# Packing two heads into 4-byte words for the transposes of q, with decay rates through the array, spare matmuls at the start and half-width last stores

## The chip, the cores and the metric

The kernel runs on one core of one Trainium2 chip. The metric is the device time of one execution in microseconds (us). A profile gives, for one execution, a span that is about 1.9 us shorter than that time. In the text PE is the matmul engine (TensorE), PEld its weight load, DVE is VectorE, ACT is ScalarE, POOL is GpSimd and SP is the engine that issues the loads and stores. "The array" is PE's array.

## The reference

An attention without a softmax over scores, followed by a gated recurrence. Sizes: 8 batches, 8 heads, 576 rows, 64 columns a head; 512 model columns and 512 inner columns. The layout changes are cut.

```python
q_s = exp(q - max) / sum over the 64 columns        # per row and head
k_s = exp(k - max) / sum over the 576 rows          # per column and head
kv  = einsum('bhsd,bhse->bhde', k_s, v)             # 64 x 64 per head
x   = einsum('bhsd,bhde->bhse', q_s, kv)            # then (batch, row, 512)
val, gate = split(x @ w_in)                         # 512 -> 512 + 512
h = exp(A_log) * h + val[:, t]                      # scan over the rows, per batch
out = (silu(gate) * ys) @ w_out
```

## The kernel before

All work is written down as one list of operations, `ORDER`. Each engine takes its own operations from it in that order, so a wait of one operation holds all later ones of that engine. A token such as `norm/P.2.0` is the operation `norm` on POOL for batch 2, part 0. Buffers are rings: a tile's memory is free when the tile so many places back has been read.

The rows of all batches are one sequence of 4608, cut into nine chunks of 512. Chunk 0 needs x of batch 0, chunk 1 needs x of batches 0 and 1, chunk 2 of batches 1 and 2. For each batch the steps are: load q, k, v; exponent of q and k on ACT (`expq`, `expk`); sums of q on DVE (`qsum`); normalization (`norm`); transposes on PE (`transp`) and their copy out of PSUM (`tevac`); k times v (`kv`), normalized on DVE (`kvn`); x products (`xa` twice, `xr` for the last rows) with copies into `xT`. For each chunk: projections (`val`, `gate`), `scan` on DVE, `tanh` on ACT, two products, output matmuls and stores.

```python
RINGS = {"qf": 2, "kf": 2, "vf": 2, "eq": 2, ..., "tp": 1, "ax": 1, "pp": 3, "po": 2, ...}

def lalog(self, e):      # 512 reads of 4 bytes
    nc.sync.dma_start(out=alog, in_=moe_A_log.rearrange("(m p) -> p m", p=128))

def expq(self, e, b, q2):
    nc.scalar.activation(buf("eq", b)[:, q2].rearrange("p c h d -> p h c d"),
        buf("qf", b)[:, 2*q2:2*q2+2].rearrange("p h (c d) -> p h c d", c=C), AF.Exp)

def transp(self, e, b, g):
    tp = buf("tp", (b, g))
    src = buf("eq", b).rearrange("p q c h d -> p (q c) (h d)")
    for j in range(6):
        nc.tensor.transpose(tp[:, j, :], src[:, 6*g + j, :], ident)      # bf16, 128 x 128

def xa(self, e, b, q2):                     # "ax": one accumulation buffer of two banks
    xp, kvc, eqT = buf("ax", (b, q2)), buf("kvc", b), buf("eqT", b)
    for h2 in range(2):
        for hp2 in range(2):
            r = slice(hp2*64, hp2*64 + 64)
            nc.tensor.matmul(xp[h2*64:h2*64+64, hp2, 0:C*PA]...,
                             lhsT=kvc[r, h2, q2, :], rhs=eqT[r, q2, :, h2, 0:PA], ...)

def scan(self, e, i, m):
    nc.vector.tensor_tensor_scan(buf("y", (i, m)), a, buf("pp", ("v", i, m)), init, ...)

for op in ORDER.split():                    # engines take their work in this order
    ...
# ... (the rest is cut)
```

## Time and profile before

| | before |
|---|---|
| time, median of 3 runs | 149.74 us (149.5 to 150.08) |
| span of the profile | 147.8 us |
| first projection | 22.63 us |
| first projection of chunk 2; PE is full from here | 53.85 us |
| end of the last matmul | 144.07 us |

The profile's page gives busy time and slices; the prediction below shows the lines that carry it. Each line says: source line, engine, operation, what it writes and reads, size, count, then busy us, mean ns of one, and idle time of the engine just before.

```profile
L265 PE MATMUL tp<-ident,eq 128*128 128x128 bf16 x144 | 13.8, 238 | 14.9 <-POOL eq L257 11.0
...
L229 ACT ACTIVATE eq<-qf 128x1152 bf16<-128x1152 f32 x16 | 18.2, 1163 | 7.1 <-DMA qf<-in_q_dram 7.1
```

The mean of a transpose, 238 ns, is not what one costs: six of them follow each other in 0.34 us, 56 ns each. An exponent of q (1152 elements per partition) takes ACT 1163 ns. The starts of the first sixteen projection matmuls (512 columns) are 427 ns apart from 23.0 to 27.3 us, and 216 ns apart from 27.6 us on.

### The profile page before, as it was taken

The numbers are of one execution on the slowest core, as the hardware profiler recorded it, in microseconds if no ns is written. First come the engines' busy times: TensorE is split into PE (matmuls) and PEld (weight loads), VectorE is DVE, ScalarE is ACT, GpSimd is POOL, SyncE is SP. The second block draws the span as 40 slices with busy tenths as digits, with TensorE's granted clock in tenths as the row PEclk, the third lists the DMA queues.
The fourth block names the chain that finished last, engine by engine and source line by source line (L and its number), as shares of the span: only waits on it lengthen the run. The fifth ranks groups of instructions, "written<-read, shape, count | busy, mean of one in ns | idle before, by whom it ended". The sixth has DMA issues, their size and how long they took to land.

```text
span 147.8 us, 3234 instructions
## 1 busy us (share of the span) xinstructions
PE 122.9 (83%) x1312; PEld 62.7 (42%) x1312; DVE 118.5 (80%) x141; ACT 101.5 (69%) x142; POOL 92.9 (63%) x77
## 2 busy tenths in 40 slices
PE   0022498949696999999999999999999999999990
PEld 0011353423352445445446776644534444444430
DVE  0498773899896798999989998897998999998510
ACT  3619756799696789799898978898555224444641
POOL 2050760979999999999998997893430660153300
PEclk9999999999999999999999999999999999999998
DMA  4999999999999999999999996000703042305296
GB/s 131 409 394 390 325 398 390 388 391 389 390 392 392 391 391 391 399 397 395 405 399 408 398 395 258 4 0 0 282 6 142 0 176 108 146 0 205 81 343 227
DMA packets 19887, 41.11 MB, mean 278 GB/s; under 512 B 1440, under 2 KB 1440, under 8 KB 19872
## 3 DMA queue, kind: packets, MB, share of 16 engines
q1 hardware_dynamic: 19872, 40.90, 74.0%
q8 instruction: 10, 0.16, 0.4%
q14 instruction: 5, 0.04, 0.1%
HBM read 31.46 MB, written 9.44 MB: 277 GB/s over the span
## 4 chain that ended last, share of the span: by engine, by line
PE 59%; DMA 16%; DVE 8%; POOL 7%; ACT 5%; issue 2%; SPq 1%; ACTq 0%
PE pp L356 32%; PE po L390 18%; DMA qf<-in_q_dram 16%; PE tp L265 3%; POOL eq L257 3%; ACT eq L229 3%; DVE y L370 2%; PE ax L317 2%; DVE z L382 2%; DVE qs L249 2%; PE ax L278 2%; POOL vb L186 2%; POOL z L382 1%; DVE u L378 1%; PE pp L390 1%
## 5 line engine op out<-in xcount | busy, mean ns | idle before, releaser
L356 PE MATMUL pp<-xT,win 128*128 128x512 bf16 (+1 forms) x320 | 70.8, 367 | 1.6 <-ACT xT L184 0.7
L382 POOL TENSOR_TENSOR z<-u,y 128x512 bf16<-128x512 f32 x28 | 35.8, 1298 | 25.8 <-DVE u L378 16.1
L356 PEld LDWEIGHTS <-win 128*128 128x128 bf16 x320 | 30.5, 99 | 33.3 <-issue 5.9
L370 DVE TENSOR_TENSOR_SCAN y<-decay,y,pp 128x512 f32<-128x512 f32 x32 | 40.4, 1271 | 2.6 <-PE pp L356 2.5
L390 PE MATMUL po<-wout,z 128*128 128x512 bf16 x136 | 34.0, 379 | 1.1 <-POOL z L382 0.9
L257 POOL TENSOR_TENSOR eq<-eq,qs 128x1152 bf16<-128x1152 bf16 x14 | 29.9, 2150 | 7.1 <-DVE qs L252 5.9
L375 ACT ACTIVATE th<-pp 128x512 f32<-128x512 f32 x36 | 21.4, 600 | 17.3 <-PE pp L356 16.0
L378 DVE SCALAR_TENSOR_TENSOR u<-th,pp 128x512 f32<-128x512 f32 x36 | 24.1, 677 | 4.5 <-ACT th L375 3.7
L265 PE MATMUL tp<-ident,eq 128*128 128x128 bf16 x144 | 13.8, 238 | 14.9 <-POOL eq L257 11.0
L249 DVE TENSOR_REDUCE qs<-eq 128x36 f32<-128x2304 bf16 (+1 forms) x10 | 20.5, 2054 | 6.2 <-ACT eq L229 6.2
L229 ACT ACTIVATE eq<-qf 128x1152 bf16<-128x1152 f32 x16 | 18.2, 1163 | 7.1 <-DMA qf<-in_q_dram 7.1
L186 POOL CAST vb<-vf 128x1152 bf16<-128x1152 f32 (+1 forms) x14 | 15.9, 1162 | 9.9 <-DMA vf<-in_v_dram 9.9
L184 ACT ACTIVATE ob<-po 128x512 f32<-128x512 f32 x27 | 16.0, 600 | 7.8 <-PE po L390 7.8
L390 PEld LDWEIGHTS <-z 128*128 128x128 bf16 x144 | 13.5, 98 | 16.3 <-POOL z L382 1.8
L265 PEld LDWEIGHTS <-eq 128*128 128x128 bf16 x144 | 10.4, 106 | 19.6 <-POOL eq L257 11.7
L235 ACT ACTIVATE ek<-kf 128x2304 bf16<-128x2304 f32 (+1 forms) x10 | 17.3, 1734 | 0.0
L184 ACT ACTIVATE xT<-ax 128x1008 bf16<-128x1008 f32 (+1 forms) x12 | 11.8, 982 | 3.1 <-PE ax L300 2.1
L184 ACT ACTIVATE eqT<-tp 128x768 bf16<-128x768 bf16 x14 | 11.4, 814 | 1.0 <-PE tp L265 1.0
L278 PE MATMUL ax<-vb,ek 64*64 64x65 bf16 x576 | 7.3, 199 | 2.0 <-POOL vb L186 1.8
L278 PEld LDWEIGHTS <-ek 64*64 64x64 bf16 x576 | 6.2, 112 | 4.3 <-issue 2.4
L370 DVE TENSOR_TENSOR_SCAN y<-acol,pp 128x512 f32<-128x512 f32 x4 | 4.8, 1214 | 3.2 <-ACT decay L184 2.4
L382 DVE TENSOR_TENSOR z<-u,y 128x512 bf16<-128x512 f32 x8 | 7.0, 885 | 0.1
(37 smaller groups left out, 67.8 us busy)
## 6 DMA issues: line engine op xcount, KB each, us to landing
out_dram<-ob SPq DMA_DIRECT2D x16, 512.0 KB, 3.2
qf<-in_q_dram SPq DMA_DIRECT2D x7, 1152.0 KB, 13.3
kf<-in_k_dram SPq DMA_DIRECT2D x7, 1152.0 KB, 12.6
vf<-in_v_dram SPq DMA_DIRECT2D x7, 1152.0 KB, 12.5
y<-in_moe_w_in_dram SPq DMA_DIRECT2D x8, 256.0 KB, 11.2
qf<-in_q_dram SPq DMA_DIRECT2D x2, 576.0 KB, 4.3
kf<-in_k_dram SPq DMA_DIRECT2D x2, 576.0 KB, 8.0
vf<-in_v_dram SPq DMA_DIRECT2D x2, 576.0 KB, 10.3
```

The costliest lines, as they stand in the source:

```text
L184: nc.scalar.activation(out, in_, AF.Copy)
L186: eng[e].tensor_copy(out, in_)
L229: nc.scalar.activation(buf("eq", b)[:, q2].rearrange("p c h d -> p h c d"), buf("qf", b)[:, 2 * q2:2 * q2 + 2].rearrange("p h (c d) -> p h ...
L249: nc.vector.tensor_reduce(s[:, 0, n].rearrange("p (a o) -> p a o", o=1), buf("eq", b)[:, h].rearrange("p q c h d -> p (q c h) d"), axis=AX ...
L257: eng[e].tensor_tensor(x, x, r.rearrange("p (a o) -> p a o", o=1) .broadcast_to([128, 2 * C, D]), ALU.mult)
L265: nc.tensor.transpose(tp[:, j, :], src[:, 6 * g + j, :], ident)
L356: nc.tensor.matmul(dst[:, a:z], lhsT=win[:, kt, col:col + 128], rhs=xT[:, kt, s0:s0 + z - a], start=(kt == 0), stop=(kt == 3))
L370: nc.vector.tensor_tensor_scan(buf("y", (i, m)), a, buf("pp", ("v", i, m)), init, op0=ALU.mult, op1=ALU.add)
L375: nc.scalar.activation(buf("th", (i, m)), buf("pp", ("g", i, m)), AF.Tanh, scale=0.5)
L378: nc.vector.scalar_tensor_tensor(buf("u", (i, m)), buf("th", (i, m)), 1.0, buf("pp", ("g", i, m)), op0=ALU.add, op1=ALU.mult)
L382: eng[e].tensor_tensor(buf("z", i)[:, m], buf("u", (i, m)), buf("y", (i, m)), ALU.mult)
L390: nc.tensor.matmul(self._po(i, r), lhsT=buf("z", i)[:, m, r * 128:(r + 1) * 128], rhs=wout[:, m], start=(m == 0), stop=(m == NM - 1))
```

## The change

The intent has five parts.

1. Two heads are interleaved, so that two bf16 values are one 4-byte word. One transpose then moves two heads: 72 transposes of 4 bytes instead of 144 of 2 bytes. ACT's exponent of q writes with a step of 4 bytes, and the x products read with that step.
2. The decay rates are loaded as four rows of 512 bytes (`lalog`) and turned by a small transpose (`talog`).
3. The factor 0.5 moves from the conversion of w_out to the output copies.
4. 37 spare matmuls on zeros (`warm`) are to keep the array busy until the first chunk.
5. The order is new: gates of chunk 0 first, all of w_in loaded ahead of batch 1's k and v. One of the last output groups is stored in two halves.

The core of the diff (the list of operations is cut to its beginning):

```diff
-lq.0.1 lq.0.0 expq.0.1 expq.0.0 lk.0.1 lq.1.- lv.0.0 lk.0.0 expq.1.1 lwin.0.0 qsum.0.1 norm/P.0.1
+lq.0.1 expq.0.1 lalog lq.0.0 qsum.0.1 expq.0.0 lq.1.- qsum.0.0 lv.0.0 lk.0.0 expq.1.1 lv.0.1
+norm/D.0.0.3 norm/P.0.6.9 expq.1.0 warm warm warm warm talog warm warm warm warm warm warm warm
 ...
-"eq": ([128, 2, C, 2, D], BF16), "eqT": ([128, 2, C, 2, PH], BF16), "tp": ([128, 6, 128], BF16)
+"eq": ([128, C, 2, D, 2], BF16), "eqT": ([128, C, 2, PH, 2], BF16), "tp": ([128, 3, 128], F32)
-    nc.sync.dma_start(out=alog, in_=moe_A_log.rearrange("(m p) -> p m", p=128))
+    nc.sync.dma_start(out=alog, in_=moe_A_log.rearrange("(m p) -> m p", p=128))
+def talog(self, e):
+    nc.tensor.transpose(buf("ax", "al")[:, 0, 0:NM], alog, ident[0:NM, 0:NM])
 ...
-    for j in range(6):
-        nc.tensor.transpose(tp[:, j, :], src[:, 6 * g + j, :], ident)
+    src = buf("eq", b).rearrange("p c h d q -> p (c h d q)").bitcast(F32)
+    for j in range(3):
+        nc.tensor.transpose(tp[:, j, :], src[:, c * 128:c * 128 + 128], ident)
-    lhsT=kvc[r, h2, q2, :], rhs=eqT[r, q2, :, h2, 0:PA],
+    lhsT=kvc[r, h2, q2, :], rhs=eqT[r, :, h2, 0:PA, q2],
+def warm(self, e):
+    nc.tensor.matmul(spare, lhsT=zero[:, 0:128], rhs=zero, start=True, stop=True)
-    copy(e, buf("ob", (i, r // 2))[:, r % 2], self._po(i, r))
+    nc.scalar.activation(dst, src, AF.Copy, scale=0.5)      # or tensor_scalar on DVE
```

## The prediction

> **What bounds the kernel now.** I read the shares of busy time first, then the slices, then the chain of work that ended last, then busy time by stretch, and last TensorE (PE) in order of time up to 60 us.
>
> ```profile
> PE 122.9 (83%) x1312; PEld 62.7 (42%) x1312; DVE 118.5 (80%) x141; ACT 101.5 (69%) x142; POOL 92.9 (63%) x77
> ...
> PE   0022498949696999999999999999999999999990
> ...
> PEclk9999999999999999999999999999999999999998
> ...
> PE 59%; DMA 16%; DVE 8%; POOL 7%; ACT 5%; issue 2%; SPq 1%; ACTq 0%
> ```
>
> PE is the busiest engine and full from slice 14 (about 50 us) to the end; the chain is 59% PE. So there are two stages: a start up to about 50 us in which PE has holes, and a rest that is as long as PE's own work.
>
> ```profile
> 30.00:35.00 5.00, 3.33 (x27) 1.30 (x28) 4.68 (x8) 4.54 (x9) 4.13 (x6) 1.00 1.07 393
> 35.00:40.00 5.00, 3.76 (x23) 1.71 (x21) 4.91 (x7) 3.88 (x5) 5.00 (x3) 1.00 1.05 388
> 40.00:45.00 5.00, 4.61 (x31) 2.24 (x28) 4.43 (x4) 5.00 (x8) 5.00 (x4) 1.00 1.05 391
> 45.00:50.00 5.00, 3.62 (x84) 1.77 (x84) 2.72 (x7) 3.55 (x5) 5.00 (x4) 1.00 1.05 391
> 50.00:60.00 10.00, 9.95 (x141) 4.96 (x139) 9.36 (x11) 8.61 (x13) 10.00 (x9) 1.00 1.05 393
> ```
>
> Columns after the stretch: its length, busy us of PE, PEld, DVE, ACT, POOL, then clock, DMA share, GB/s. From 30 to 50 us PE lacks 4.7 us, while the DMA engines run at 390 GB/s without a break and POOL is full. After 50 us PE lacks almost nothing, and DVE is at 9.4 of 10: the next bound lies close.
>
> ```profile
> 22.63 6.01 PE L356 MATMUL pp<-xT,win 128*128 128x512 bf16 x16 [0.75 <-ACT xT L184]
> ...
> 48.77 1.90 PE L356 MATMUL pp<-xT,win 128*128 128x512 bf16 x8
> ...
> 53.85 2.75 PE L356 MATMUL pp<-xT,win 128*128 128x512 bf16 x12
> ```
>
> The first sixteen projection matmuls take 6.01 us, 376 ns each; twelve at 53.85 take 2.59 us to the next start, 216 ns each. So the first chunk ran on a slow array, although the clock line shows 9 throughout: that line does not show this slowness.
>
> In the chain in order of time (start, us, what), PE alone carries the end:
>
> ```profile
> 2.22 8.31 DMA qf<-in_q_dram
> ...
> 62.31 0.34 PE tp L265 x6
> 62.64 0.34 PE ax L317 x4
> 62.98 0.97 PE po L390 x4
> 63.95 0.86 PE pp L356 x4
> ...
> 143.19 0.88 PE pp L390 x4
> 144.07 0.02 issue
> 144.09 0.60 ACT ob L184
> ```
>
> This gives unit costs on a full PE: 0.34 us for a group of six transposes, 0.34 for one of four x matmuls, 0.86 for four matmuls of 512 columns. The first line gives q of batch 1 landing at 10.53 us.
>
> [...] 12 x 427 + 4 x 216 = 5.99 us against 6.01. [...] No run of before has a 4-byte transpose: open. [...] The new moving reads step 4 bytes, [...] I expect no slowing; before shows no such read. [...] DVE's copies of 768 elements take 545 ns[...].
>
> **The change part by part.**
>
> *Transposes.* Before: 144 of 128x128 in bf16, six to a group, 24 groups, 0.34 us a group in the chain, 56 ns each: 24 x 0.34 = 8.2 us of PE. After: 72 of 4 bytes, three to a group. If one costs 56 ns too, a group is 0.17 us and 4.1 us go; [...] 24 x 0.67 = 16 us, 8 us more than before. I take 80 ns: 0.24 us a group, saving 2.4 us, of which some 17 of 24 groups lie in the full stage: 1.7 us.
>
> *Copies out of the transposes.* ACT: 128x512 takes 600 ns and 128x1008 1012, so 0.83 ns an element; 384 words cost 600 - 128 x 0.83 = 494 ns against 814. 19 groups instead of 14: 9.4 us against 11.4. DVE: [...] 5 groups instead of 10, 2.7 us less. Off the path except at the start.
>
> *Normalisation.* POOL does 1152 elements in 2150 ns, 1.87 ns each; now 16,896 elements instead of 16,128: 31.5 us against 30.1. The new pattern has rows of two elements; I assume the same rate.
>
> *Scale 0.5 moved.* POOL's two w_out conversions took 2768 ns each at a time when POOL was full (33.5 and 42.1 us); a plain cast of 512 takes 612 ns, so 1024 about 1.15: 3.2 us off POOL before the first output matmul. The copies out of PSUM get a factor at no cost I can see.
>
> *Decay rates.* 512 scattered 4-byte reads become four rows of 512 bytes. The 15 to 20 us stretch moved 350 GB/s instead of 390: 5 x 40 = 0.2 MB, 0.5 us of DMA saved.
>
> *Spare matmuls.* 33 of them. Twelve cold matmuls x (427 - 216) = 2.5 us in the first chunk, about 0.5 us more in early kv and x matmuls. The cost is PE time in holes.
>
> *Other order.* DVE gets fewer z multiplies (6 against 8, 0.885 us each) but 8.5 output copies against 7 (0.68), small x copies and a clearing of zeros: two fewer z are -1.8 us, 1.5 outputs +1.0, five fewer transpose copies -2.7, normalising 768 instead of 1152 elements twice -1.2, two more w_in casts +0.8, one more first-batch x copy +0.8, four small copies +1.0, the zeros +0.3. That sums to -1.8, 116.7 us against 118.5; I allow up to 122, since several of these could run slower on strided pairs.
>
> *When the full stage starts.* q of batch 1 landed at 10.53 us with 2.95 MB queued up to it; at 0.39 MB per us that is 7.6 us plus 2.9 fixed. After the change batch 0's k is the end of 4.7 MB (q0, q1, v0, k0): 15.0 us; with q2 and the four gate pieces of w_in (0.26 MB each) 6.95 MB: 20.7 us. Loads now put q of three batches, k and v of batch 0, all of w_in and then k, v of batch 1 first: 10.4 MB. Before had moved 10.4 MB by 29.6 us (sum of the first eight slices), so v of batch 1 lands at about 30.5 us. Then q3, v2, k2 (3.5 MB at 0.39 MB per us = 9 us) bring batch 2 at about 39.5, and q4 with w_out (2.2 MB) at about 45. Batch 0's k ends near 15 us: exponent 1.15, kv 0.7, kvn 0.6, x matmuls 0.5, two copies 1.3, so x at about 19.5; the gate half of w_in is there at 20.7 plus a 0.6 cast. First chunk: 21.3 us against 22.63, with 8 x 0.86 = 6.9 us on PE but 4 x (1.22 + 0.68) = 7.6 on DVE plus one qsum: done near 30 instead of 37. Chunk 1 starts when batch 1 has gone through k exponent, kv, x and its copy (3.5 us): 34, done about 42. Before ended it at 50.6. Then w_out at 45 plus casts: first outputs and chunk 2 at about 47, against 53.85 before.
>
> *Sum.* Before, 53.85 to the last matmul's end at 144.07 is 90.2 us of full PE. After has from 47 us the same, less 1.7 for transposes, plus two output groups not yet done (2 x 0.86): 90.2. So PE ends at 137.2. The tail after it was 147.8 - 144.07 = 3.7 us and stays (the half-width stores serve rows 3 of the last chunk, while the last store is whole again): 140.9. I add 0.5 us for holes, and the time is 149.74 - 147.8 = 1.9 us above the span: 143.3; I say 143.2. DVE check: by 47 us its order has five qsums (14.5 us), eight scans (9.8), eight gate products (5.4), three kvn (1.8) and about 9 of the rest, 41 us; so at most 81 are left in 90: 90% busy, it holds.
>
> **The rivals.** (1) 4-byte transposes [...]: 8 us more PE, nearly all in the full stage, about 149 or more. For: nothing in this trace measures them. [...] (2) DVE becomes the bound: up to 122 us plus 5.7 before its first input, 5 of tail and the 6.8 us it idled between 20 and 50 (30 less 23.2 busy): 139.5 of span, 141.4 of time, and every new wait of DVE adds to it. For: 9.4 of 10 busy already. (3) DMA hides the better start: the same bytes must land, 390 GB/s to 88 us; if batches 1 and 2 come later than I hold, chunk 2 starts at 50 and the time is 146. (4) Strided work slows POOL's normalisation or PE's x reads (14 groups of 0.34 us, doubled 4.8 us): 146 to 148. (5) Everything is kept full: PE could start its full stage at 43, giving 139.
>
> **Range and chances.** The centre is 143.2. Rival 5 sets the low end, 138.5; rivals 3 and 4 the high end, 148. Faster by over 2% means below 146.8: all of 2 and 5, most of 3. Rival 1 has perhaps one chance in ten. Faster 0.82, same 0.13, slower 0.05.
>
> **What would show it.** Right: 12 to 16 early projection matmuls at 216 ns; the first projection near 21 us; chunk 2 near 47 us; a transpose group at 0.17 to 0.33 us from its start to the next instruction's; ACT's copy near 0.49 us; PE full from about 47 us with little idle; DVE between 116 and 122 us busy. Wrong: transpose groups above 0.5 us; x groups above 0.34; POOL normalisation of 1536 elements above 3 us; PE idle behind DVE after 50 us, which would mean the freed start is given back later.

## The result

| | before | after |
|---|---|---|
| time, median of 4 runs each | 149.62 us (149.39 to 150.08) | 148.64 us (148.53 to 148.93) |
| span of the profile | 147.8 us | 146.8 us |
| first projection | 22.63 us | 23.54 us |
| first projection of chunk 2 | 53.85 us | 51.58 us |
| end of the last matmul | 144.07 us | 142.59 us |

A ratio here is taken over the fast runs of both kernels; it is not quite the ratio of the medians. It is 0.9934, with a 95% interval of 0.9905 to 0.9963: about 0.7% faster, so within 2%. The prediction said 143.2, and its range ended at 148.0. A second job on another chip gave 148.99 us and 0.9944.

The page of the changed kernel, in the same places as the prediction shows for before (busy time, the slices of PE, the engines' shares of the chain):

```profile
PE 131.5 (90%) x1267; PEld 66.1 (45%) x1282; DVE 116.4 (79%) x144; ACT 100.9 (69%) x140; POOL 93.8 (64%) x80
...
PE   5785979784998999999999999999999999999980
...
PE 66%; DMA 20%; ACT 7%; DVE 2%; issue 1%; SPq 1%; ACTq 0%; DVEq 0%
```

PE's early digits are now the spare matmuls (12.9 us of the 131.5). DVE is at 116.4 us, as predicted (116.7). But DMA's part of the chain has grown from 16% to 20%. Busy time by stretch, columns as in the prediction:

```profile
35.00:40.00 5.00, 3.42 (x24) 1.57 (x18) 3.93 (x5) 5.00 (x5) 3.97 (x4) 0.66 1.05 392
40.00:45.00 5.00, 4.69 (x91) 2.31 (x89) 4.59 (x8) 4.23 (x5) 4.41 (x3) 1.00 1.05 389
...
50.00:60.00 10.00, 9.95 (x127) 5.05 (x127) 8.50 (x12) 9.52 (x14) 9.41 (x7) 1.00 1.06 392
```

After 50 us PE is full again. Between 35 and 40 us it is not: it waits, and the array has gone slow once more. The clock column says 0.66, and the weight loads of the matmuls from 39.08 to 39.93 start 0.42 us apart, against 0.216 us in chunk 0. PE in order of time shows why (start, busy us, what, and in brackets the idle time before and what ended it):

```profile
23.54 2.75 PE L364 MATMUL pp<-xT,win 128*128 128x512 bf16 x12 [0.34 <-ACT xT L191]
...
33.12 0.78 PE L286 MATMUL ax<-vb,ek 64*64 64x65 bf16 x72 [0.55 <-POOL vb L193]
...
36.39 0.50 PE L325 MATMUL ax<-eqT,kvc 64*64 64x504 bf16 x4 [1.24 <-DVE xT L193]
...
37.94 3.70 PE L364 MATMUL pp<-xT,win 128*128 128x512 bf16 x11 [0.22 <-issue]
...
51.58 2.75 PE L364 MATMUL pp<-xT,win 128*128 128x512 bf16 x12
```

The first projections are at the fast rate from the start: twelve take 2.6 us, 216 ns each. Chunk 0 ends at 32.3 us, 5 us earlier than before. But then batch 1's x is not there: k times v at 33.12, the second x product only at 36.39 because DVE must first copy the first one out of the single buffer, and chunk 1's first two projection matmuls at 37.94. The others wait for ACT's copy of the second product until 38.70. In the kernel before, the same chain ran between 28.6 us (k times v) and 35.7 us (end of the second copy), beside chunk 0's gates. The chain that ended last, in order of time, says what held ACT's copy:

```profile
21.62 13.27 DMA qf<-in_q_dram
34.97 2.83 ACT eq L238 x2
37.80 0.86 ACT xT L191
38.70 2.09 PE pp L364 x6
```

ACT's queue has the exponents of batch 3 ahead of the copy, and they waited for batch 3's q, which landed at about 34.9 us. The first projection, too, stood behind exponents. Batch 0's x products were done at 21.15 us, but ACT copied two of them only behind the exponents of batch 2, which had waited for their q; the second copy, from 22.84 us on, ended at 23.49:

```profile
19.62 2.85 ACT L238 ACTIVATE eq<-qf 128x1152 bf16<-128x1152 f32 x2 [0.98 <-DMA qf<-in_q_dram]
22.33 0.63 ACT L191 ACTIVATE xT<-ax 128x576 bf16<-128x576 f32 x1
```

Last, the two groups that answer to those shown of before:

```profile
L238 ACT ACTIVATE eq<-qf 128x1152 bf16<-128x1152 f32 x16 | 23.4, 1493 | 7.6 <-DMA qf<-in_q_dram 7.5
...
L273 PE MATMUL tp<-ident,eq 128*128 128x128 f32 x72 | 13.6, 302 | 2.2 <-POOL eq L265 2.0
```

The exponent with the 4-byte step takes 1493 ns instead of 1163. What a group of three 4-byte transposes costs on a full PE is read from its start to the start of the next instruction:

```profile
61.00 0.55 PE L273 MATMUL tp<-ident,eq 128*128 128x128 f32 x3
61.38 1.03 PE L364 MATMUL pp<-xT,win 128*128 128x512 bf16 x4
```

Such gaps are 0.32 to 0.42 us. Over the twelve groups between 52 and 103 us they sum to 4.40 us, and in the kernel before, with six bf16 transposes to a group, twelve groups sum to 4.40 us too. The packing saves PE nothing. Of the 24 groups only these twelve lie in the full stage.

### The profile page after: what moved, and what is told of

The parts are those of the page before. It is cut to its first block, busy times and chain, and to the rows that moved or that the text cites. A ratio compares the mean times of both kernels' runs of the same rounds, so it can differ in the third digit from the quotient of the medians.

```text
span 146.8 us, 3190 instructions
## 1 busy us (share of the span) xinstructions
PE 131.5 (90%) x1267; PEld 66.1 (45%) x1282; DVE 116.4 (79%) x144; ACT 100.9 (69%) x140; POOL 93.8 (64%) x80
## 4 chain that ended last, share of the span: by engine, by line
PE 66%; DMA 20%; ACT 7%; DVE 2%; issue 1%; SPq 1%; ACTq 0%; DVEq 0%
PE pp L364 37%; PE po L409 20%; DMA qf<-in_q_dram 20%; ACT eq L238 4%; PE tp L273 3%; PE ax L286 2%; PE ax L325 2%; ACT ek L242 1%; PE pp L409 1%; DVE y L382 1%; PE pp L347 1%; ACT xT L191 1%; DVE u L390 0%; ACT ob L416 0%; ACT th L387 0%
## 5 line engine op out<-in xcount | busy, mean ns | idle before, releaser
L394 POOL TENSOR_TENSOR z<-u,y 128x512 bf16<-128x512 f32 x30 | 38.7, 1301 | 22.7 <-DVE u L390 14.3
L265 POOL TENSOR_TENSOR eq<-eq,qs 128x768 bf16<-128x768 bf16 (+1 forms) x16 | 32.6, 2043 | 13.4 <-DVE qs L260 8.7
L238 ACT ACTIVATE eq<-qf 128x1152 bf16<-128x1152 f32 x16 | 23.4, 1493 | 7.6 <-DMA qf<-in_q_dram 7.5
L256 DVE TENSOR_REDUCE qs<-eq 128x36 f32<-128x2304 bf16 x6 | 15.3, 2546 | 3.1 <-ACT eq L238 3.1
L273 PE MATMUL tp<-ident,eq 128*128 128x128 f32 x72 | 13.6, 302 | 2.2 <-POOL eq L265 2.0
L370 PE MATMUL spare<-zero 128*128 128x512 bf16 x35 | 12.9, 513 | 1.5 <-DVE zero L161 1.2
L273 PEld LDWEIGHTS tp<-ident,eq 128*128 128x128 f32 x72 | 9.0, 152 | 8.4 <-POOL eq L265 3.3
L191 ACT ACTIVATE eqT<-tp 128x384 f32<-128x384 f32 x19 | 9.4, 493 | 2.4 <-PE tp L273 2.2
L259 DVE TENSOR_REDUCE qs<-eq 128x18 f32<-128x1152 bf16 x4 | 5.3, 1336 | 5.7 <-ACT eq L238 5.7
L325 PE MATMUL ax<-eqT,kvc 64*64 64x504 bf16 x56 | 5.8, 402 | 2.0 <-DVE xT L193 1.2
L418 DVE TENSOR_SCALAR ob<-po 128x512 f32<-128x512 f32 x8 | 5.4, 679 | 2.3 <-PE po L409 2.3
## 6 DMA issues: line engine op xcount, KB each, us to landing
kf<-in_k_dram SPq DMA_DIRECT2D x2, 576.0 KB, 10.9
```

Of the source, the lines that this page charges most:

```text
L191: nc.scalar.activation(out, in_, AF.Copy)
L238: nc.scalar.activation(dst, src, AF.Exp)
L265: eng[e].tensor_tensor(x, x, r.broadcast_to([128, 2 * (c1 - c0), D, 2]), ALU.mult)
L273: nc.tensor.transpose(tp[:, j, :], src[:, c * 128:c * 128 + 128], ident)
L394: eng[e].tensor_tensor(buf("z", i)[:, m], buf("u", (i, m)), buf("y", (i, m)), ALU.mult)
```

## The experiments

All kernels ran beside the kernel before on the same chip. "After" is the changed kernel. Times are medians of all timed runs; the ratio to before, with its 95% interval in brackets, is taken over the fast runs alone. One run each of e5, e6 and e10 was slow, all others were fast. I first held theory C: the packing buys nothing, and what is missing is the late start of chunk 1, set by the chain behind chunk 0 on engines with a fixed order. Its rival L was that the landings of batch 1's data hold it.

**e1: the packing alone undone.** Layouts, exponent, transposes and x reads as before, six bf16 transposes to a group; everything else, the order too, as after.

```diff
-"tp": ([128, 3, 128], F32)      # and eq, eqT interleaved
+"tp": ([128, 6, 128], BF16)     # and eq, eqT as in the kernel before
```

> The changed kernel with only the packing undone: 144 transposes in bf16, six to a group in place of three 4-byte ones; order, loads, spare matmuls and everything else stay. Theory T (the packing saves PE nothing, as a group takes 0.33 us in the changed kernel against 0.34 before, and it makes the exponent of q slower, 1.49 against 1.16 us each): PE's groups 0.34 us, exponent of q back at 1.16 us, ACT 18.6 instead of 23.4 us for it, ACT copies 0.81 instead of 0.49; time between 147.0 and 148.6 us, so the same or a little faster than the changed kernel. Rival R (the packing is worth what was hoped, 2 to 4 us, and is hidden by something else): 150 us or more without it.

147.84 us, 0.9894 (0.9829 to 0.9959). The same kernel on another chip (r2, below): 148.62 us, 0.9918 (0.9887 to 0.995). ACT's exponent is back at 1158 ns, and twelve transpose groups in the same window sum to 4.42 us. From the place where PE is full to the last matmul both kernels need the same: 89.8 us here in both profiles, 90.0 in both profiles of after. So the packing gives the full stage nothing. The time lies where theory T had it. Both medians lie below after's, but the intervals overlap: that undoing it gains a little is likely and not shown.

**e2: no spare matmuls.**

```diff
-... warm warm warm warm talog warm warm ...
+... talog ...
```

> The changed kernel without its 33 spare matmuls. If they do what they are for, the first twelve to sixteen projection matmuls run at 427 ns, the granted clock falls below 0.95 over 0 to 30 us and the first chunk ends about 2.5 us later; by theory T the delay is partly absorbed, since chunk 1 waits for loads and the x copy until 38 us: 148.6 to 150.0 us. Rival: the clock does not matter for the end at all (148.6, within 0.2).

149.46 us, 0.9997 (0.9939 to 1.0055). The first 28 projections took 8.30 us, 296 ns each on average, instead of 216:

```profile
22.54 8.30 PE L361 MATMUL pp<-xT,win 128*128 128x512 bf16 x28 [0.27 <-ACT xT L188]
```

That is 28 x 80 ns = 2.2 us more in chunk 0; by the ratios of e2 and after, some 0.9 us of it reached the end, with intervals that overlap. In its profile the input stream was also faster than in after (393 GB/s from 4 to 8 us against 337; what that is worth is seen in r2 and e15 below), so the spare matmuls may be worth more than that.

**e7: the kernel before with spare matmuls alone (37 of them).**

```diff
+warm x16 before transp.0.2, x4 before transp.0.0, x8 before transp.0.1, x2 before kv.0.0,
+x4 before kv.0.1, x3 before val.0.1
```

> The kernel before with nothing but 37 spare matmuls in the idle stretches of the matmul engine ahead of chunk 0. Theory: the first 16 projections, 6.0 us in the kernel before, take 3.6 us, but the second half of chunk 0 waits for weights that VectorE and GpSimd cast at 32.5 us, so the gain at the start of chunk 2 is under 0.7 us and the kernel ends at 149.1 to 149.7. Rival (the slow clock at the start is itself what the kernel before loses): 2.0 us or more earlier, at or below 147.7.

150.07 us, 1.0024 (0.9978 to 1.0069): no gain, somewhat above the range of the theory. The first sixteen projections were done at 26.6 us instead of 28.6, and then PE waited for weights:

```profile
32.36 3.04 PE L361 MATMUL pp<-xT,win 128*128 128x512 bf16 x7 [1.23 <-POOL win L191]
```

The seven after that wait of 1.23 us took 435 ns each: PE was slow again. Here the spare matmuls gained nothing, since PE then stood for weights that POOL had yet to cast.

**e3: the decay rates loaded and turned later.**

```diff
-lq.0.1 expq.0.1 lalog lq.0.0 ...        (talog among the spare matmuls)
+lalog behind lk.0.1, talog ahead of acol
```

> The changed kernel with the load of the decay rates moved from second place to after the first k and v loads, and its transpose moved to just before its use. In the changed kernel the DMA engines moved 290 to 364 GB/s from 3.5 to 9 us, before it about 410, and the second half of q arrives 1 us later (7.01 against 6.02 us). If the small load of four rows causes that, the rate from 3.5 to 9 us goes back to about 410 and the second exponent starts near 6.1 us; the stream gains 0.9 us and the time falls by 0.3 to 0.9 us. Rival: the slow stretch comes from elsewhere (loading q twice in a row), rate unchanged, time unchanged within 0.2 us.

148.74 us, 0.9935 (0.9879 to 0.999): no change. The input stream was faster at first (407 GB/s from 4 to 8 us against after's 337), but the later turn of the rates held ACT's queue (its exponent of the rates waited 1.25 us for PE, and the exponents of batch 0's k stand behind it), and the first projection came at 24.92.

**e8: one store again whole.**

```diff
-outp.8.3.0 outp.8.3.1 oevac/D.8.3.0 oevac/A.8.3.1 store.8.3.0 store.8.3.1
+outp.8.3 oevac/D.8.3 store.8.3
```

> The changed kernel with only the split of the first of the last four output groups undone (one product of full width, one copy, one store of 256 KB). Theory: that group isn't the last to be stored, so nothing moves: within 0.2 us of the changed kernel, 148.4 to 148.9. Rival (the half-width stores shorten the end): 0.3 us or more slower, at or above 149.0.

148.46 us, 0.9916 (0.9879 to 0.9954). The half-width stores do nothing that can be seen.

**e4: ACT's copy of batch 1's x ahead of batch 3's exponents.**

```diff
-... expq.3.1 ... expq.3.0 ... xaevac/A.1.1
+... xaevac/A.1.1 expq.3.1 expq.3.0
```

> The changed kernel with the exponents of q of batch 3 moved on ACT from ahead of the copy of the second x piece of batch 1 to behind it. In the changed kernel that copy waits in ACT's order for the load of q of batch 3, which lands at 34.9 us, and ends at 38.65; the projections of chunk 1 start then. If this order holds the start back: the copy starts at 36.9 us, chunk 1 at 37.9, 0.8 us sooner, time 0.3 to 1.0 us lower. Rival: chunk 1 is early but the exponents then come late and batch 3 pays it back: time the same or up to 0.5 us longer.

153.03 us, 1.0199 (1.0147 to 1.025): the expectation was wrong. The copy began 0.7 us earlier, but DVE's queue has the sums of batch 3 ahead of chunk 1's scans, and those now waited for the later exponents (first line DVE, second PE):

```profile
40.75 2.55 DVE L256 TENSOR_REDUCE qs<-eq 128x36 f32<-128x2304 bf16 x1 [3.84 <-ACT eq L238]
...
44.87 3.57 PE L364 MATMUL pp<-xT,win 128*128 128x512 bf16 x8 [3.17 <-DVE y L382]
```

The scans hold the three projection buffers, so PE stood for 3.17 us and then ran slow (446 ns a matmul). The queues are coupled: one of them can't be reordered alone.

**e6: the second x product in two banks of its own, its copy on DVE.** The two banks of the output rows are free at that time.

```diff
-xa.1.0 ... xaevac/D.1.0 xa.1.1 xrevac/D.1 ... xaevac/A.1.1
+xa.1.0 xb.1.1 ... xaevac/D.1.0 xrevac/A.1 ... xbevac/D.1.1.0 xbevac/D.1.1.1
```

> The changed kernel, but the second x product of batch 1 goes into the two accumulation banks of the output rows (free at that time) directly behind the first, and its copy runs on VectorE, in two halves, behind the first copy; ScalarE takes the small copy of the remaining rows. Theory C (the single accumulation buffer and ScalarE's queue behind the exponents of batch 3 make up 1 to 2 us of the late start): the second product starts near 35.0 instead of 36.4, its copy ends near 37.6 instead of 38.6, chunk 1 starts near 37.8 instead of 38.7, and the kernel ends 0.6 to 1.0 us earlier, near 147.9. Rival D (the vector engine's order is what counts, since the sums of batch 3 stand ahead of the scans): chunk 1 starts earlier, but the first scan of it, now at 40.5, comes no earlier, the matmul engine waits for it, and the end moves by less than 0.3 us.

149.36 us, 0.994 (0.9864 to 1.0015); one of the four runs was slow, and the median of the three fast ones is 149.0. Chunk 1 started earlier, as theory C had it, and then lost it, as rival D had it:

```profile
37.44 2.31 PE L381 MATMUL pp<-xT,win 128*128 128x512 bf16 x9 [0.21 <-DVE xT L193]
41.83 3.50 PE L381 MATMUL pp<-xT,win 128*128 128x512 bf16 x8 [2.08 <-DVE y L399]
```

The first scan of chunk 1 came at 40.60, against 40.71 in after.

**e13: half of DVE's sums (a wrong result).** The sums of q of batches 2 to 4 read only 32 of 64 columns.

```diff
+                if b in (2, 3, 4):
+                    src = src[:, :, :, 0:D // 2]
                 nc.vector.tensor_reduce(s[:, 0], src, axis=AX.X, op=ALU.add)
```

> The changed kernel, but VectorE sums only 32 of each 64 exponents of q for batches 2, 3 and 4 (a wrong result on purpose): three reductions of 2.55 us become about 1.3, so 3.8 us of VectorE's work between 22 and 50 us go, 1.2 of them directly ahead of chunk 1's first scan (now at 40.7). Theory D (VectorE's queue is the bound of this stretch): chunk 2 starts 2 us earlier and the kernel ends at 147.0 or below. Rival C (the chain from chunk 0's end to chunk 1's projections is the bound, and VectorE's time is only spread along it): the first scan comes 1 us earlier, chunk 1's projections start where they did, and the end moves by less than 0.7 us.

148.95 us over 20 runs, 0.9944 (0.9927 to 0.9961): nothing. The first scan came at 39.87 instead of 40.71, but PE was no earlier, and its next wait was for another engine:

```profile
43.98 0.78 PE L288 MATMUL ax<-vb,ek 64*64 64x65 bf16 x72 [0.76 <-ACT ek L242]
```

So DVE's load alone is not the bound either: rival D, called theory D in this expectation, falls too in this form.

**e14: chunk 1's projections read batch 0's x (a wrong result).** They wait for nothing of batch 1; all work and all orders stay.

```diff
-            t0 = i * W % RX
+            t0 = 0 if i == 1 else i * W % RX
```

> The changed kernel, but chunk 1's projections read the x of batch 0 (a wrong result on purpose), so they wait for nothing of batch 1; every engine keeps all of its work and its order. Theory C (the x chain of batch 1 is what chunk 1 waits for): chunk 1's first projection comes directly behind the last piece of x work in the matmul queue, near 37.4 instead of 38.7, and the end about 1 us earlier, near 147.8; the rest of the chain stays because those products stand ahead in the same queue. Rival D (VectorE's sums and scans): chunk 1 starts earlier but then waits for scans, and the end moves by less than 0.4 us.

148.64 us, 0.9924 (0.9897 to 0.9952): theory C expected 147.8, and it fails here. The eleven projections of chunk 1 ran at once, and PE then stood for the scans, as rival D had it (the end to move by less than 0.4 us):

```profile
37.43 2.54 PE L364 MATMUL pp<-xT,win 128*128 128x512 bf16 x11
41.52 1.89 PE L364 MATMUL pp<-xT,win 128*128 128x512 bf16 x8 [1.54 <-DVE y L382]
```

**e9: no waits for landings of batch 1's k and v and batch 3's q (a wrong result).** Those three read a table in SBUF; all loads stay in place.

```diff
-            nc.scalar.activation(buf("ek", b)[:, h], buf("kf", b)[:, h], AF.Exp)
+            src = decay[:, :, 0:C * D] if b == 1 else buf("kf", b)     # likewise v of 1, q of 3
+            nc.scalar.activation(buf("ek", b)[:, h], src[:, h], AF.Exp)
```

> The changed kernel with every load in place, but the exponent of k and the cast of v of batch 1 and the exponent of q of batch 3 read a table that lies in SBUF since 28 us (a wrong result on purpose), so nothing between chunk 0 and chunk 1 waits for a landing. Theory L (landings hold chunk 1 back, as the prediction had it, only later): chunk 1's first projection, at 38.7, comes 2 to 4 us earlier and the kernel ends near 145.5. Theory C (the in-order chain behind chunk 0 holds it: the products with values at 33, normalization, x product, VectorE's copy, second x product into the same buffer, ScalarE's copy, and VectorE's sums of batch 3 ahead of the first scan): it comes 0.5 to 1.0 us earlier, because only the 0.6 us wait for v and the 1.0 us wait for q go, and the kernel ends at 147.7 to 148.2.

149.64 us, 0.9989 (0.9939 to 1.0039): no gain in the timed runs. Theory L (145.5) and theory C (147.7 to 148.2) both missed. In the profile the wait for v is gone, and the wait for the single buffer stays:

```profile
33.77 1.00 PE L289 MATMUL ax<-vb,ek 64*64 64x65 bf16 x72
...
37.25 0.41 PE L328 MATMUL ax<-eqT,kvc 64*64 64x504 bf16 x4 [1.23 <-DVE xT L193]
```

This execution started late (first projection 24.80, chunk 0 done at 33.51). From there to the full stage it took 1.2 us less than after, and the late start, 1.3 us, took that back. So some 1 us hung on these landings, not the 2 to 4 us of theory L, if the profile is taken by itself. The other three runs were slower still (149.54 to 150.85); why isn't shown.

**e5: batch 1's k is not loaded (batch 1 uses k of batch 0).** This takes 1.18 MB out of the stream, so that later landings can come up to 2.9 us earlier (an estimate from the bytes and some 400 GB/s; after's slices show 386 to 403 from 11 to 88 us). It was meant to give a wrong result; with these inputs the result passed all the same.

```diff
-lk.1.-
-            nc.scalar.activation(buf("ek", b)[:, h], buf("kf", b)[:, h], AF.Exp)
+            nc.scalar.activation(buf("ek", b)[:, h], buf("kf", 0 if b == 1 else b)[:, h], AF.Exp)
```

> The changed kernel, but K of batch 1 is never loaded and batch 1 uses K of batch 0 (a wrong result on purpose: 1.18 MB, about 2.9 us of the stream of inputs, are taken away ahead of the landing of v of batch 1). Theory L (the landing of batch 1's data is what holds chunk 1 back, so the prediction's only fault was to put that landing 1.4 us too early): v of batch 1 lands near 29.0 us instead of 31.9, the products with values of batch 1 start 2 us or more earlier, chunk 1's first projection comes near 36 instead of 38.7, and the kernel ends 2 to 2.5 us earlier, near 146.3. Theory C (what holds it back is the chain of steps behind those products, on engines whose order is fixed, with one accumulation buffer for the two halves): the data is there but the matmul engine reaches those products only after chunk 0's projections, near 32.3, chunk 1 starts near 38.0, and the kernel ends 0.5 to 1.0 us earlier, near 147.9.

147.78 us, 0.9846 (0.9785 to 0.9907); one of four runs, the profiled one, was slow, and the median of the three fast ones is 147.46. That lies between the two expectations, nearer to that of theory C, about 1.3 us below after by the ratios, with intervals that just touch. So the stream as a whole seems to count. Which waits became shorter isn't shown, since the only profile is of the slow run.

**r1: after once more.**

```diff
+# unchanged, run again
```

> The changed kernel itself once more, on the chip of the other runs of this call. Expected: 148.4 to 149.0 us, 0.7% faster than the kernel before. In its first profile the input stream ran at 320 to 370 GB/s between 4 and 10 us, in the profiles of three variants at 390 to 410. If that comes from the kernel, it will be there again with the first projection near 23.5; if it is chance, the stream runs at 390 or more here or in others and the start moves by up to 1 us with it.

148.99 us, 0.9944 (0.9928 to 0.9961). The slow stretch of the input stream was there again: 277 GB/s from 4 to 8 us.

**e10 and e11: two other orders, both wrong.**

```diff
-ORDER of after
+two orders with transposes of batch 2 between chunk 0's projections (e11: also e6's two banks)
```

> The changed kernel with the packing undone (bf16 transposes, six per group) and another order of the same work in the first 52 us: batch 1's v loaded ahead of k as before, but one weight load earlier, transposes of batch 2 between chunk 0's projections, the scans of chunk 1 grouped, the last transposes of batch 3 and one GpSimd normalization after chunk 1. Theory C (order and engine load set the start of chunk 2, now 51.6): chunk 2 starts near 50.0 and the kernel ends near 146.5, 1.2 us below the run with the packing undone alone (147.84). Rival: the start is at its limit by the input stream, and the end stays at 147.5 to 148.2.

> The same idea as the other order, but with the second x product of batch 1 in the two output banks, its copy in two halves, and the sums of batch 3 in two halves, with an order made for that. Theory C: chunk 1 starts about 1 us earlier than in the changed kernel (near 37.7) and, since VectorE's sums no longer stand in one piece ahead of the scans, keeps it: chunk 2 near 50.2, end near 146.5. Rival D (VectorE is full in this stretch, so an earlier chunk 1 only waits for its scans, as in the run with two banks alone): no better than 147.5.

154.48 us (1.0272) and 149.71 us (0.9983), both with wrong results. My orders had some transposes ahead of the normalization of the same data. Nothing follows from them.

**e12 and r2: such an order with that mended, and its base.** r2 is e1 unchanged.

```diff
-ORDER of after, ring of one for all x products
+first 52 us reordered, two banks as in e6, sums of batch 3 in halves; bf16 transposes as in e1
```

> The changed kernel with the packing undone, the second x product of batch 1 in two banks, the sums of batch 3 in two halves, and an order of the first 52 us made for that, this time with every normalization ahead of its transposes (correct results expected). Theory C (order and the hand-over between engines set the start of chunk 2): chunk 1 near 37.5, chunk 2 near 50.5, end 0.5 to 1.0 us below its base r2. Rival W (the four engines are so full between 20 and 52 us that no order gains): within 0.4 us of r2, and slower if the matmul clock drops again.

> The changed kernel with only the packing undone, once more, on the chip of the other runs of this call. Expected as in its first run: 147.8, 0.7% below the changed kernel, 1.1% below the kernel before.

e12: 148.72 us, 0.9939 (0.9916 to 0.9962), correct. r2: 148.62 us, 0.9918 (0.9887 to 0.995). The order gained nothing against r2, and its stream was the faster one (392 GB/s from 4 to 8 us); rival W stands for this attempt. r2 against e1 was the useful finding. The same kernel started in two ways: stream at 400 GB/s from 4 to 8 us, span 145.6, and stream at 317, span 146.5.

**e15 and e16: the 2 KB load of the decay rates issued first instead of second.** e15 is after with that one move, e16 is e1 with it.

```diff
-lq.0.1 expq.0.1 lalog lq.0.0 ...
+lalog lq.0.1 expq.0.1 lq.0.0 ...
```

> The changed kernel with one line moved: the 2 KB load of the decay rates is issued first instead of second. Theory P (its place between the first loads of q slows the stream): 390 GB/s or more from 4 to 8 us, the first projection near 22.6 instead of 23.4 to 24.4, and the kernel ends 0.7 to 1.0 us earlier, 147.7 to 148.2. Rival (chance, or something else in the changed kernel): the stream runs at 280 to 360 GB/s again and the time stays at 148.5 to 149.0.

> The same move in the kernel with the packing undone. Theory P: first projection near 21.9 in every run, 147.2 to 147.8 us with little scatter, the best of all versions. Rival (chance): 147.5 to 149.3 as the two runs of that kernel so far.

e15: 147.74 us (147.69 to 148.59), 0.9877 (0.9854 to 0.9901). e16: 147.60 us (147.35 to 147.82), 0.9854 (0.9831 to 0.9877). Both are below before and after, with intervals that don't overlap; e16 has the lowest ratio of all kernels that do the whole work, though its interval overlaps that of e15. In the profiles the last matmul of e15 starts 0.6 us earlier than after's; the other 0.3 us of its shorter span lie behind that. The stream ran at 383 and 398 GB/s (last column, after first and e15 second):

```profile
4.00:8.00 4.00, 3.43 (x9) 1.37 (x10) 1.62 (x2) 2.48 (x2) 0.00 (x0) 1.00 0.98 337
4.00:8.00 4.00, 3.37 (x15) 1.33 (x13) 1.56 (x3) 2.98 (x2) 0.00 (x0) 1.00 1.03 383
```

Three lines of after, POOL's cast of batch 1's v, DVE's sums of batch 3 and its first scan of chunk 1:

```profile
31.93 1.15 POOL L193 CAST vb<-vf 128x1152 bf16<-128x1152 f32 x1 [1.15 <-DMA vf<-in_v_dram]
...
37.83 2.55 DVE L256 TENSOR_REDUCE qs<-eq 128x36 f32<-128x2304 bf16 x1 [1.07 <-ACT eq L238]
...
40.71 1.18 DVE L382 TENSOR_TENSOR_SCAN y<-decay,y,pp 128x512 f32<-128x512 f32 x1
```

and the first and last of these in e15, with ACT's exponents of batch 3 between them:

```profile
31.32 1.15 POOL L192 CAST vb<-vf 128x1152 bf16<-128x1152 f32 x1
...
34.36 2.84 ACT L237 ACTIVATE eq<-qf 128x1152 bf16<-128x1152 f32 x2
...
40.11 1.18 DVE L381 TENSOR_TENSOR_SCAN y<-decay,y,pp 128x512 f32<-128x512 f32 x1
```

All three come 0.6 us earlier: the cast of v, the exponents (34.97 in after) and the scan. The expected early first projection did not come in e15 (23.94; the clock column says 0.51 from 16.1 to 18 us, where after has 1.00), and it did in e16 (22.42). The exponents, the sums and the scan of e1, without the packing:

```profile
34.31 2.22 ACT L240 ACTIVATE eq<-qf 128x1152 bf16<-128x1152 f32 x2 [0.72 <-DMA qf<-in_q_dram]
36.56 2.55 DVE L258 TENSOR_REDUCE qs<-eq 128x36 f32<-128x2304 bf16 x1 [0.46 <-ACT eq L240]
...
39.45 1.18 DVE L383 TENSOR_TENSOR_SCAN y<-decay,y,pp 128x512 f32<-128x512 f32 x1
```

The profiles side by side, in us, with the stream in GB/s:

| kernel | stream 4 to 8 us | first projection | chunk 0's projections end | first scan of chunk 1 | last matmul starts | span |
|---|---|---|---|---|---|---|
| before | 407 | 22.63 | 37.19 | 36.81 | 143.03 | 147.8 |
| after | 337 | 23.54 | 32.25 | 40.71 | 141.55 | 146.8 |
| r1 (after again) | 277 | 24.36 | 33.06 | 41.28 | 142.75 | 147.6 |
| e15 (after, rates first) | 383 | 23.94 | 32.65 | 40.11 | 140.97 | 145.9 |
| e1 (bf16) | 400 | 21.85 | 31.33 | 39.45 | 140.61 | 145.6 |
| r2 (bf16 again) | 317 | 23.47 | 32.36 | 40.51 | 141.52 | 146.5 |
| e16 (bf16, rates first) | 398 | 22.42 | 31.45 | 39.61 | 140.77 | 145.8 |
| e6 (two banks) | 330 | 23.79 | 32.50 | 40.60 | 143.05 | 147.9 |
| e9 (no landings) | 305 | 24.80 | 33.51 | 40.73 | 141.63 | 147.1 |
| e13 (half sums) | 294 | 24.11 | 32.81 | 39.87 | 142.26 | 147.1 |
| e14 (other x) | 316 | 24.05 | 32.76 | 40.28 | 141.99 | 147.0 |

With the rates second, the stream was slow (277 to 356 GB/s) in 12 of 14 profiles, e10 and e11 among them; the other two, e1 and e2, had 400 and 393. With the rates elsewhere (before, e7, e3, e12, e15, e16) it was at 383 to 407 in all six.

## Why the prediction was wrong

The prediction's sum, term by term, against the profile of after:

| term | predicted | measured |
|---|---|---|
| first projection | 21.3 | 23.5 |
| chunk 0 done | 30 | 32.3 |
| chunk 1 starts | 34 | 37.9, in full 38.7 |
| chunk 2 starts | 47 | 51.6 |
| from there to the last matmul's end | 90.2 | 91.0 |
| tail, with 0.5 for holes in the prediction | 4.2 | 4.2 |
| time above the span | 1.9 | 1.8 |
| time | 143.3 | 148.6 |

- **The start is the main fault: 4.6 of the 5.4 us.** The step that failed is "Chunk 1 starts when batch 1 has gone through k exponent, kv, x and its copy (3.5 us): 34". That adds up durations as if each engine were free. v of batch 1 was in POOL's hands at 31.9 (predicted landing: 30.5), and the path from there took 6.0 us to the first and 6.8 to the remaining projections. It holds the cast of 1.15 us, which the sum left out, the wait of 1.24 us for the single x buffer, and ACT's exponents of batch 3 ahead of the last copy. 2.2 us of the lateness were there already when chunk 0 ended, since the first projection itself was 2.2 us late: there, too, copies of x stood behind exponents in ACT's queue (to 22.47 us), and the sum had let them follow at once.
- **Why it isn't one cause.** Removing the waits for landings (e9), the wait for the buffer (e6), half of DVE's sums (e13) or the dependence on batch 1's x (e14) brought nothing each in the timed runs, and another order (e12) neither. e9 is the weakest of these, as its profile did save 1.2 us and lost them to a late start. Each time PE's next wait was for another engine: scans in e6 and e14, ACT in e13. From 32 to 50 us several chains of nearly the same length run side by side. That is argued from these misses together; no run removed several at once. What went with an earlier end is the stream that feeds all chains: shifted by 0.6 us in e15, or by up to 2.9 us in e5, it moved the end by about 1 us.
- **One of these chains can be read off the profiles.** In the ten fast profiles that keep the packing and all sums (after, r1, e2, e3, e4, e6, e8, e9, e14, e15), the first scan of chunk 1 comes 5.73 to 5.77 us after ACT begins the exponents of batch 3: two exponents, DVE's sums, a reciprocal. In after the exponents had waited 1.04 us for their q; in e3, e9 and e15 ACT came to them without a wait, 1.5 to 1.7 us after chunk 0's projections. From that scan to the start of the last matmul it is 100.8 to 100.9 us in after, e3, e8, e9 and e15, and longer in the others. The prediction has nothing of it in chunk 1's 3.5 us, though the chain of the kernel before has two of these steps one behind the other (29.14, ACT's exponents of q, 2.23 us; 31.39, DVE's sums, 2.56). It isn't the only bound: e13 cut it by 1.0 us, and PE then waited for ACT's exponent of k.
- **A cost of the change that nobody looked for.** "Decay rates: ... 0.5 us of DMA saved" holds for the old load. But the new load, as second in the queue, goes with a slower stream, and moving it to first place was worth 0.9 to 1.0 us (e15 against after and r1, by the ratios). Moved behind the first k and v (e3) it gave the fast stream but no time. So part of rival 3 came true, by a route that the prediction did not have: landings came later not because of the bytes but because of the rate at 4 to 8 us. How a 2 KB load does that stays open.
- **The transposes: the term was mis-sized.** "I take 80 ns: 0.24 us a group": measured 0.32 to 0.42 us a group with neighbours, no saving in twelve groups. The 80 ns were the author's estimate; no profile of before has a 4-byte transpose. At the lower end, 0.33 us for three, one costs about 110 ns, and a 2-byte one 56 ns (0.34 us for six): the same for each byte. Nor do 17 of the 24 groups lie in the full stage, but twelve. Of the 1.7 us that were booked for the full stage, 0.8 us show as a longer stage; some 0.4 us of the rest is one more group that was already done when it began (12 instead of before's 11), and what made up for the other 0.5 was not taken apart. Rival 1, a group at 0.67 us (an estimate: three transposes at four times the 56 ns of before's), did not come on a full PE.
- **ACT's exponents** were not in the sum: 16 x (1493 - 1163) = 5.3 us more on ACT, 0.29 ns for each of the 1152 elements. By the ratios of e1, r2 and e16 against after, r1 and e15 the whole packing cost 0.2 to 0.7 us at the end, with intervals that overlap. Two of the exponents lie in the chain above: from their start to the first scan it is 5.13 or 5.14 us in e1, r2 and e16, 0.6 us less than with the packing.
- **Right were** the fast first projections (216 ns), x reads with the step of 4 bytes at no cost (groups stay near 0.34 us), ACT's copy of a transpose group (493 ns against 494), DVE's (550 ns for 384 words, 545 for 768 bf16 values in before), POOL's conversion of w_out (1040 ns against 1150), the factor 0.5 at no cost (679 ns on DVE either way), DVE's sum (116.4 against 116.7), and a full PE from chunk 2 on. The 13 us from chunk 1 to chunk 2 (12.9 from the first full projection) came out by luck: chunk 1 was to take 8 us (34 to 42) and the rest was to be a wait for w_out, but it took 10.9 us, to 49.6, and the outputs followed at once, at 49.85. Rival 2 did not come: PE had no idle behind DVE that counts after 52 us.
- **The spare matmuls** (37 in the order; the prediction counted 33) did what they were for in chunk 0 (216 ns a projection, 296 without them): e2 lost some 0.9 us without them, by ratios whose intervals overlap. The 2.5 us booked for the first chunk came nearly whole there (2.2). Up to 1.3 us were lost again behind it, after PE had waited 0.55, 0.76 and 1.24 us: eleven projections in 3.70 us at 37.94, where 216 ns each would be 2.4 (the wait for the second copy, until 38.70, is in the 3.70). That those waits made the array slow there is the author's reading; no run filled them.

## What to carry to other kernels

When a stage is fed by a stream and worked by several engines in fixed order, predict its end by walking each engine's queue, not by adding the durations along one path: what stands ahead in the same queue counts, and so does a buffer that exists once. If taking one cause away gains nothing, look for chains of equal length and try what feeds all of them; an interval between two steps that stays the same in every profile is such a chain. Before packing data for fewer instructions, measure one instruction of the new width, and the engine that has to write the new layout.
